# Dummy matmuls of 128 columns instead of 256 in front of the first attention scores

## The chip, the cores and the metric

The kernel runs on one core of a Trainium2 chip. The metric is the time of one execution in device microseconds (us). A profiled execution also has a span, from its first to its last recorded instruction, which is about 1.7 us shorter than its time. Ratios are the mean time of one kernel's fast runs over that of the other's of the same rounds, so they are not quite the ratio of the medians quoted. The line numbers L286, L472 and so on are the kernel's own; all kernels here keep them.

## The reference

Causal attention with 16 extra "beacon" keys and values per head, then a two-layer network with a squared relu:

```python
# q, k, v: (8 batches, 8 heads, 576 tokens, 64); beacon_k, beacon_v: (8, 8, 16, 64)
k_all = concat([beacon_k, k]); v_all = concat([beacon_v, v])
scores = q @ k_all.T / 8          # causal mask on the part of k
out = softmax(scores) @ v_all
x = out as (4608 tokens, 512)
h = relu(x @ w_in)                # w_in 512 x 2048
return (h * h) @ w_out            # w_out 2048 x 512, float32
```

## The kernel before

The kernel plans itself before it emits anything: a small simulator walks over all operations with guessed durations and fixes the order of each engine. Where TensorE has nothing ready before 22 us of simulated time, the simulator puts a dummy matmul ("fill"), whose guessed length is 107 ns whatever its size. The order is then frozen, and TensorE keeps to it on the chip: in all ten profiles without a reordering its 3114 other matmuls come in the same sequence of lines.

```python
if best is None:                                   # nothing ready on this engine
    if e == "PE" and 0.3 < now < self.FILL_UNTIL and self.pools["ps"]:
        cols = 128 if now < 4.0 else 256
        free[e] = now + 0.107
        issued.append((Op("fill", "PE", 0.107, lambda e, cols=cols, bank=...: self.fill(bank, cols)), e, now))
...
def emit_fill(bank, cols):                          # L286
    nc.tensor.matmul(ps[bank][:, 0:cols], g[1][:, 0, 0:128], g[1][:, 0, 0:cols], start=True, stop=True)
```

Batch 0's q and k arrive head pair by head pair. Pair 0 comes in two pieces by way of a float32 buffer and a cast (their transposes are L472). Pairs 1 to 3 of batch 0, and all of batch 1, are loaded by GpSimd's queue with a cast on the way (issue L440) and transposed by TensorE (L475). The order of that queue is fixed too:

```python
SOFT = "t0 p1k p1q t1 p2k p2q v0 v1 p3k p3q v2 v3 v4 w0 w1 w2 w3".split()   # p: pair, v: value block, w: quarter of w_in
...
strided[1, 0, 0, "k"].behind[:] = chain[-1:]        # batch 1's first k comes after w3
```

The other lines that matter here: L611 scores, L620 exp, L715 attention times v, L878 first layer of the network, L894 and L896 relu, L903 square, L916 second layer, L318 casts and copies.

The softmax here doesn't subtract the row's maximum and nothing guards it: scores larger than these inputs give would overflow.

## Time and profile before

| | |
|---|---|
| time, median of the first 3 runs | 340.99 us (340.25 to 341.39) |
| execution that was profiled | 342.69 us, span 341.0 us |
| TensorE busy | 335.6 us, 98% |
| dummy matmuls | 83, of which 32 with 128 and 51 with 256 columns |

The profiled execution took longer than any of the timed ones. The rows on which the argument rests are in the prediction. They are rows of the timeline (start, duration, engine, line, operation, output<-inputs, and in brackets the idle time before them with what ended it) and of the chain that ended last (start, duration, what).

### The profile page before, as it was taken

The page shows a single profiled execution, that of the slowest core. Times are in us where ns is not written, and L with a number is a line of the kernel's source. Part 1 is how long each engine was busy: PE and PEld are TensorE (multiplying, and loading weights), DVE is VectorE, ACT ScalarE, POOL GpSimd, SP SyncE. Part 2 cuts the span into 40 slices and gives each one's busy share as a digit, 9 for nine tenths or more (in the row PEclk, how much of TensorE's full clock was granted, in tenths as well). Part 3 has the DMA queues.
Part 4 walks back from the last instruction along what each step waited for, and adds up shares of the span by engine and source line. Part 5 has one row for each costly group of instructions (what it writes and reads, how often), then busy time and mean ns, then how long its engine had stood idle before and what let it go on. Part 6 is the DMA issues. An engine that isn't in the chain of part 4 may idle for free.

```text
span 341.0 us, 7787 instructions
## 1 busy us (share of the span) xinstructions
PE 335.6 (98%) x3197; PEld 187.4 (55%) x3197; DVE 173.0 (51%) x389; ACT 190.3 (56%) x270; POOL 92.5 (27%) x145
## 2 busy tenths in 40 slices
PE   8999999999999999999999999999999999999996
PEld 7677665544564555555467855545454544444444
DVE  3886886238465982477336743767255502401400
ACT  2886765367647765576456653675367316514721
POOL 9773712406504533042315041504000000000000
PEclk9999999999999999999999999999999999999999
DMA  8999987999999999799989998997310131011003
GB/s 143 209 185 213 209 149 165 224 241 217 170 204 238 219 172 189 162 238 188 201 154 220 226 215 131 217 233 125 105 62 2 29 104 62 0 60 65 0 2 123
DMA packets 143953, 51.72 MB, mean 152 GB/s; under 512 B 130702, under 2 KB 138798, under 8 KB 143918
## 3 DMA queue, kind: packets, MB, share of 16 engines
q1 hardware_dynamic: 135375, 42.19, 61.8%
q0 software_dynamic: 7904, 8.69, 15.0%
q8 instruction: 25, 0.41, 0.5%
q10 hardware_dynamic: 639, 0.36, 0.4%
q14 instruction: 10, 0.08, 0.1%
HBM read 37.22 MB, written 9.44 MB: 137 GB/s over the span
## 4 chain that ended last, share of the span: by engine, by line
PE 97%; DVE 1%; issue 0%; ACT 0%; DVEq 0%
PE ps L878 36%; PE ps L916 36%; PE ps L715 9%; PE strip L611 9%; PE ps L286 3%; PE ps L475 2%; PE ps L782 1%; PE ps L828 1%; DVE g L903 1%; PE ps L472 0%; ACT g L894 0%; PE ps L420 0%; DVE g L896 0%; ACT osb L316 0%; DVE g L292 0%
## 5 line engine op out<-in xcount | busy, mean ns | idle before, releaser
L878 PE MATMUL ps<-xT,w_in 128*128 128x512 bf16 (+3 forms) x704 | 134.0, 340 | 0.7 <-DVE g L896 0.7
L916 PE MATMUL ps<-w_out,g 128*128 128x512 bf16 x560 | 131.4, 379 | 0.0
L620 ACT ACTIVATE pt<-strip 128x1024 bf16<-128x1024 f32 (+3 forms) x107 | 101.9, 1000 | 43.2 <-PE strip L611 42.8
L878 PEld LDWEIGHTS <-w_in 128*128 128x128 bf16 x704 | 65.5, 98 | 52.9 <-issue 2.0
L894 ACT ACTIVATE g<-ps 128x512 bf16<-128x512 f32 (+2 forms) x120 | 67.5, 563 | 45.2 <-PE ps L878 44.7
L903 DVE TENSOR_TENSOR g<-g 128x1024 bf16<-128x1024 bf16 (+2 forms) x80 | 54.2, 684 | 68.6 <-ACT g L894 67.7
L916 PEld LDWEIGHTS <-g 128*128 128x128 bf16 x560 | 51.0, 98 | 54.8 <-issue 1.7
L318 POOL CAST qk_area<-stg 128x512 bf16<-128x512 f32 (+2 forms) x60 | 40.1, 676 | 66.1 <-DMA stg<-in_q_dram 33.7
L318 POOL CAST vb<-stg 128x512 bf16<-128x512 f32 (+1 forms) x40 | 26.4, 671 | 67.8 <-DMA stg<-in_v_dram 49.3
L316 ACT COPY osb<-ps 128x512 f32<-128x512 f32 (+2 forms) x28 | 15.8, 567 | 50.8 <-PE ps L916 48.6
L715 PEld LDWEIGHTS <-pt 128*128 128x128 bf16 (+1 forms) x960 | 35.7, 98 | 11.0 <-issue 2.1
L715 PE MATMUL ps<-vb,pt 128*128 128x65 bf16 (+1 forms) x960 | 39.8, 194 | 0.0
L689 DVE TENSOR_TENSOR pt<-pt,tri 128x512 bf16<-128x512 bf16 x64 | 31.6, 503 | 10.2 <-ACT pt L620 9.0
L611 PE MATMUL strip<-qT,kT 64*128 64x208 bf16 (+15 forms) x596 | 34.2, 239 | 0.0
L734 DVE TENSOR_TENSOR xn<-ps,rcp 128x320 bf16<-128x320 f32 (+2 forms) x64 | 31.5, 492 | 2.3
L611 PEld LDWEIGHTS <-kT 64*128 64x128 bf16 x596 | 19.0, 94 | 21.2 <-issue 19.9
L732 DVE RECIPROCAL rcp<-ps 128x5 f32<-128x5 f32 (+2 forms) x64 | 12.2, 190 | 34.5 <-PE ps L715 34.2
L896 DVE TENSOR_SCALAR g<-ps 128x512 bf16<-128x512 f32 (+2 forms) x40 | 23.4, 601 | 8.6 <-PE ps L878 7.4
L318 DVE COPY osb<-ps 128x512 f32<-128x512 f32 (+1 forms) x10 | 6.5, 651 | 31.0 <-PE ps L916 19.0
L286 PE MATMUL ps<-g 128*128 128x256 bf16 (+1 forms) x83 | 12.0, 302 | 1.1 <-DVE warm L293 1.1
L362 POOL DMA_DIRECT2D stg<-in_v_dram x10 | 8.6, 866 | 6.4 <-DMA w_in<-in_moe_w_in_dram 5.3
L286 PEld LDWEIGHTS <-g 128*128 128x128 bf16 x83 | 7.9, 122 | 3.5 <-issue 1.5
(40 smaller groups left out, 82.2 us busy)
## 6 DMA issues: line engine op xcount, KB each, us to landing
out_dram<-osb SPq DMA_DIRECT2D x17, 512.0 KB, 4.3
stg<-in_q_dram SPq DMA_DIRECT2D x24, 256.0 KB, 5.0
stg<-in_k_dram SPq DMA_DIRECT2D x18, 256.0 KB, 5.3
stg<-in_v_dram SPq DMA_DIRECT2D x18, 256.0 KB, 4.7
w_in<-in_moe_w_in_dram POOLq DMA_DIRECT2D x4, 512.0 KB, 8.7
w_out<-in_moe_w_out_dram POOLq DMA_DIRECT2D x4, 512.0 KB, 11.2
stg<-in_v_dram POOLq DMA_DIRECT2D x6, 256.0 KB, 8.3
stg<-in_k_dram SPq DMA_DIRECT2D x6, 224.0 KB, 4.1
```

Of the source, the lines that this page charges most:

```text
L286: nc.tensor.matmul(ps[bank][:, 0:cols], g[1][:, 0, 0:128], g[1][:, 0, 0:cols], start=True, stop=True)
L318: eng[e].tensor_copy(dst, src)
L611: nc.tensor.matmul(st[:, hj, at:at + t1 - t0], kT[b % 2][hp, pr, 128 * c:128 * c + 128], qT[b % 2][hp, pr, t0:t1], start=True, stop=True,)
L620: nc.scalar.activation(pt[:, :, at:at + width], strips[qk.slots[s]][:, :, 0:width], AF.Exp, bias=0.0, scale=scale)
L689: nc.vector.tensor_tensor(out=d, in0=d, in1=tri[:, m0:m0 + m, :][:, None].to_broadcast([128, 2, m, 128]), op=ALU.min)
L715: nc.tensor.matmul(a[:, at + (t - tl[0]) * (D + 1):at + (t - tl[0] + 1) * (D + 1)], P[0:rr, hj, o:o + 128], vb[b % 2][0:rr, c, 2 * pr + hj ...
L734: nc.vector.tensor_tensor(out=xn[b % 2].rearrange("p t (h d) -> p h t d", d=D)[:, h0:h0 + nh, tl[0]:tl[0] + nt], in0=a[:, :, :, 0:D], in1= ...
L878: nc.tensor.matmul(h[:, lo - spans[0][0]:hi - spans[0][0]], w_in_sb[:, mc, ft * 128:(ft + 1) * 128], xT[:, mc, lo % RING:lo % RING + hi - lo],
L894: nc.scalar.activation(dst, h, AF.Relu, bias=0.0, scale=1.0)
L896: nc.vector.tensor_scalar(out=dst, in0=h, scalar1=0.0, scalar2=None, op0=ALU.max)
L903: nc.vector.tensor_tensor(out=d, in0=d, in1=d, op=ALU.mult)
L916: nc.tensor.matmul(o, G[:, fc, ts * 128:(ts + 1) * 128], w_out_sb[:, fc, :], start=(fc == 0), stop=(fc == NFT - 1))
```

## The change

The intent is to get real work onto TensorE sooner. A dummy that already stands in the queue must finish before real work behind it can start, so shorter dummies should delay it less. The diff is one line; in the frozen order it makes 18 dummies shorter: fifteen before the second piece's transposes and three after the first scores.

```diff
-                            cols = 128 if now < 4.0 else 256
+                            cols = 128 if now < 7.0 else 256
```

## The prediction

> **What bounds the kernel now.** I read the page first: it says what the 341 us are made of, but it cannot price a change that touches only the first 9 us.
>
> ```profile
> PE 335.6 (98%) x3197; PEld 187.4 (55%) x3197; DVE 173.0 (51%) x389; ACT 190.3 (56%) x270; POOL 92.5 (27%) x145
> L286 PE MATMUL ps<-g 128*128 128x256 bf16 (+1 forms) x83 | 12.0, 302 | 1.1 <-DVE warm L293 1.1
> ```
>
> TensorE is busy nearly all the time, so over the whole kernel its work is the bound. L286 is the dummy matmul: 83 of them. They keep TensorE occupied while the first loads come in, so the early part of "PE busy" is not work that anyone waits for, and the page cannot tell whether a shorter dummy shortens anything. For that I took the timeline of the first 10 us, where each row is start, duration, engine, instruction, and in brackets the idle time before it and what ended it.
>
> ```profile
> 4.41 0.46 PEld L472 LDWEIGHTS <-qk_area 120*128 120x128 bf16 x4
> 4.84 0.51 ACT L316 CAST qk_area<-osb 112x384 bf16<-112x384 f32 x1 [0.44 <-DMA osb<-in_q_dram]
> 5.25 2.58 PE L286 MATMUL ps<-g 128*128 128x256 bf16 x15
> 5.61 0.36 DVE L318 CAST qk_area<-osb 112x384 bf16<-112x384 f32 x1
> 7.67 0.46 PE L472 MATMUL ps<-ident,qk_area 112*128 112x112 bf16 x6
> 8.17 0.51 DVE L318 COPY kT<-ps 128x336 bf16<-128x336 bf16 x1 [1.79 <-PE ps L472]
> 8.44 0.78 ACT L620 ACTIVATE pt<-strip 128x736 bf16<-128x736 f32 x1 [3.09 <-PE strip L611]
> ```
>
> Fifteen dummies stand between the transposes of the first piece of q and k (L472 at 4.41) and those of the second (L472 at 7.67). The second piece is cast by 4.84 + 0.51 = 5.35 (ScalarE) and 5.61 + 0.36 = 5.97 (VectorE). From 5.97 to 7.67 those transposes wait for nothing but the dummies queued ahead of them: **1.70 us too late**. VectorE idles 1.79 us and ScalarE 3.09 us for it. So in this stage the dummies do bound.
>
> The next question is how far a lead made here travels. The chain that ended last, in order of time, is where I looked (start, duration, what), with the timeline's rows at the same place, and the landing times of the loads.
>
> ```profile
> 27.81 2.64 PE ps L878 x24
> 30.45 0.02 issue
> 30.47 0.41 ACT g L894
> 30.88 0.03 issue
> 30.91 0.70 PE ps L475 x24
> ```
>
> ```profile
> 30.91 0.57 PEld L475 LDWEIGHTS <-qk_area 96*64 96x64 bf16 x24 [0.77 <-DMA qk_area<-in_k_dram]
> 32.57 0.31 PEld L475 LDWEIGHTS <-qk_area 96*64 96x64 bf16 x12 [0.22 <-DMA qk_area<-in_q_dram]
> ```
>
> At 30.91 TensorE starts to transpose batch 1's k. The chain names an activation that freed a PSUM bank at 30.88; the timeline names the load. Both hold: that load was issued at 19.77 and took 11.1 us to land, 19.77 + 11.1 = 30.87. The two end within 0.01 us. The row at 32.57 is the same for q: issued at 20.44, 11.9 to land, 32.34, and TensorE idled for it too. **These two landings are a floor**: TensorE executes in program order, so nothing after 30.9 can start sooner unless batch 1's loads land sooner.
>
> **What the Trainium skill says.** "TensorE: Matmul & The Clock Gate", section "Part 1: The HAM clock gate", says the array starts at half clock and reaches full clock after a free-running window of about 3.4 us with activity, and that back-to-back matmuls start N/1.2 ns apart cold and N/2.4 + 2.5 ns warm: 107 and 213 ns cold, 56 and 109 warm, for 128 and 256 columns. The trace agrees: the 32 early dummies of 128 columns start 107 ns apart; of the fifteen with 256, seven start 213 ns apart (7 start from 5.44 to 6.72) and those from 6.9 on 109. The row of granted clocks (all 9s) does not show this; the spacing does, and the change of pace is at about 6.9 us. "Part 4: PE-mode transpose" of the same page says transposes do not count as activity in the same way; nothing in this trace tests it. "DMA: Bandwidth & Descriptors", section "Issuing engines are not separate DMA queues", says that every queue shares the same DMA engines; here their mean busy share is over 1.0 from 2 to 38 us in the stretches I asked for (1.03, 1.12, 1.11, 1.17, 1.30, 1.12) at some 180 to 230 GB/s, so the loads set their own pace.
>
> **The change part by part.** The comparison of instruction orders shows the same number of instructions on every engine, in the same order; 18 dummies change from 256 to 128 columns: all fifteen above, and the first three of the four after the first scores (8.33 us). Nothing is removed and no wait is added.
>
> 1. The fifteen. From 5.25, at 107 ns each while the clock is cold, they take 15 x 0.107 = 1.6 us: the second transposes start at about 6.85 instead of 7.67, **0.8 us sooner** (both operands have been there since 5.97, so none of this is lost yet). First scores and first exp follow: the exp at about 7.6 instead of 8.44.
> 2. The three of the next group run warm: 3 x (109 - 56) = **0.16 us**. Lead at the first pair-1 transposes: 0.97, that is 7.9 instead of 8.87.
> 3. Then the loads of batch 0's later heads take it back. Landings, as issue plus time to landing: pair 1 k at 2.39 + 4.0 = 6.4 and q at 7.2 (needed at 7.9 and 8.9: no wait); pair 2 k at 4.28 + 5.4 = 9.7 and q at 10.2 (needed at 10.97 - 0.97 = 10.0 and 10.66: just in time); pair 3 k at 7.81 + 6.9 = **14.7** and q at 8.46 + 6.8 = 15.3. Pair 3's k transposes started at 15.08 before, and would now be asked for at 14.1: they wait for 14.7. About **0.35 us** of lead is left.
> 4. Those 0.35 us pass through attention and the first hidden-layer matmuls (L878) to 30.4. There the floor at 30.87 stands: the batch-1 load is issued by GpSimd, whose work before it (casts of v, loads of w_in) waits for loads and not for TensorE. Lead left after 30.91: 30.91 - 30.87 = **0.04 us**, and after 32.57 about zero.
>
> The sum: 0.8 + 0.16 gained, 0.6 lost at 14.7, the rest lost at 30.9. What remains is 0 to 0.05 us of 341, which nobody can see against runs of 340.25 to 341.39.
>
> **The rivals.**
> - *The lead survives.* If the landing at 30.87 moved with the front (earlier casts on GpSimd, or VectorE's copies no longer colliding with GpSimd's descriptor work), 0.35 to 1 us would come through: about 340.0 to 340.6. Against it: busy DMA engines throughout, and the copies only move, they do not shrink. For it: the clock's window is free-running, so in some executions the fifteen run cold to the end (15 x 213 = 3.2 us instead of 2.4), TensorE reaches 30.9 after the landing, and there the change does gain a few tenths. This is why I put the median slightly below the old one.
> - *The clock warms later.* If 128-column dummies or the transposes that now come earlier count as too little activity, the window that closes near 6.9 fails and half clock lasts another 3.4 us. Work between 6.9 and 10.3 would then be up to twice as long, perhaps 1 us, more than the lead: TensorE arrives up to a few tenths behind the floor, 341.0 to 341.5. Against it: the first 32 dummies were 128 columns wide and just as dense, and the array is still filled without a break until 6.85.
> - *ScalarE is the bound and not the loads.* From 9.97 to 14.3 five exps run back to back. If they set the pace, the lead comes through to 14.7 as whole; pair 3's landing still stops it. Same total.
>
> **Range and chances.** Centre: 340.99 less about 0.15 for the executions with an unlucky window, 340.8. The three earlier runs spread over 1.1 us and a second chip session can shift the median by as much, so 340.1 to 341.5. Faster by 2% would need 6.8 us, seven times the whole lead; slower by 2% would need a clock that stays cold for some 14 us. Both 0.01.
>
> **What would show each step right or wrong.** In the changed kernel: (1) the fifteen dummies start 107 ns apart and the second L472 starts at 6.7 to 6.95; (2) the first exp at about 7.6; (3) L475 for pair 3 starts 0.2 to 0.5 us sooner than 15.08, with a landing at about 14.7 just before it; (4) L475 of batch 1 starts at 30.9 again, TensorE now idle longer than 0.47 us before it, the chain naming the load and no activation; from there each stage at its old time within the jitter of landings. Wrong would be: L472 of the second piece waiting for anything other than the dummies; dummies at 107 ns long after 6.9; batch 1's landing moved by more than 0.3 us, in which case the end moves with it; or a span that moves while 30.91 does not, for which I have no mechanism.

## The result, and the profile after

The changed kernel took 340.51 us in the median (340.16 to 340.65, 4 runs) beside 341.1 us for the kernel before, ratio 0.9985 with a 95% interval of 0.9966 to 1.0005: the same. It lies inside the range, 0.3 us under the centre.

The profile, however, fell from a span of 341.0 to 338.4 us, far more than the times did. These are the page's lines for the whole span of the changed kernel:

```profile
PE 333.8 (99%) x3197; PEld 186.2 (55%) x3197; DVE 172.8 (51%) x389; ACT 190.5 (56%) x270; POOL 94.3 (28%) x145
L286 PE MATMUL ps<-g 128*128 128x128 bf16 (+1 forms) x83 | 10.3, 278 | 1.1 <-DVE warm L293 1.1
```

Dummies cost 1.7 us less (10.3 for 12.0), yet the span lost 2.5 (340.95 and 338.45 before rounding). The timeline of the same execution:

```profile
5.22 1.01 PE L286 MATMUL ps<-g 128*128 128x128 bf16 x15
5.52 0.36 DVE L318 CAST qk_area<-osb 112x384 bf16<-112x384 f32 x1
6.07 0.46 PE L472 MATMUL ps<-ident,qk_area 112*128 112x112 bf16 x6
6.83 0.78 ACT L620 ACTIVATE pt<-strip 128x736 bf16<-128x736 f32 x1 [1.68 <-PE strip L611]
9.39 0.31 PEld L475 LDWEIGHTS <-qk_area 96*64 96x64 bf16 x12 [0.41 <-DMA qk_area<-in_k_dram]
10.48 0.31 PEld L475 LDWEIGHTS <-qk_area 96*64 96x64 bf16 x12 [0.60 <-DMA qk_area<-in_q_dram]
26.51 2.78 PE L878 MATMUL ps<-xT,w_in 128*128 128x240 bf16 x24
29.23 0.56 PEld L475 LDWEIGHTS <-qk_area 96*64 96x64 bf16 x24 [0.23 <-DMA qk_area<-in_k_dram]
```

There are three things to read here. First, the second transposes start at 6.07 and not 7.67: 1.6 us sooner, twice the forecast. In this execution the fifteen dummies start 56 ns apart, so the clock was already warm when they began; in the profile of the kernel before it warmed only near 6.9 us. Half of the 1.6 us is therefore the change and half is the clock's luck. Second, the loads of pair 2 (k at 9.39, q at 10.48) now stop TensorE, where it never waited before. The idle times in brackets are those of the weight loads (PEld) and are no measure of this: some 0.2 us stood in each place before without any wait (0.21 and 0.17, "issue"). The starts are a better one: the lead was 1.77 us at pair 1's k (7.10 for 8.87) and 1.15 at pair 2's q (10.48 for 11.63), so these loads cost 0.62 us. Third, batch 1's transposes started at 29.23 and not 30.91. The load itself landed at 29.17 and not at 30.87, and TensorE came to them at 26.51 + 2.78 = 29.29 (ends of matmuls are modelled), so it did not wait. I had taken that landing as fixed.

The rest of the 2.5 us is a stall further on. The timeline of the kernel before, near 39 us:

```profile
38.88 2.69 POOL L318 CAST vb<-stg 128x512 bf16<-128x512 f32 x4
38.99 2.88 DVE L903 TENSOR_TENSOR g<-g 128x544 bf16<-128x544 bf16 x3
42.27 1.03 PE L878 MATMUL ps<-xT,w_in 128*128 128x272 bf16 x8 [0.69 <-DVE g L896]
```

and of the changed kernel in its first profile:

```profile
36.94 2.91 POOL L318 CAST vb<-stg 128x512 bf16<-128x512 f32 x4
37.34 2.02 DVE L903 TENSOR_TENSOR g<-g 128x544 bf16<-128x544 bf16 x3
```

Three squares need 1.3 us when nothing disturbs them (0.44 each); beside GpSimd's casts they took 2.88 us in one execution and 2.02 in the other. In the slow case TensorE ran out of freed banks and stood still for 0.69 us. The Trainium skill, "SBUF — State Buffer", section "Who interferes with whom", says that a VectorE instruction with two SBUF inputs contends with a GpSimd instruction that reads SBUF. The square reads its input twice from SBUF and the cast reads SBUF, and these numbers agree. Up to the first L916 (46.44 before, 43.94 after) the two executions are 2.50 us apart, 1.68 of it at batch 1 and 0.82 in this stretch; from there to the end they stay 2.5 apart.

So two profiles cannot price this change. The question for the experiments was which of these differences come with the change, and how much of the front's lead reaches the end.

### The profile page after: what moved, and what is told of

Its sections match the earlier page's. It is cut to its first block, busy times and chain, and to the rows that moved or that the text cites. A ratio compares the mean times of both kernels' runs of the same rounds, so it can differ in the third digit from the quotient of the medians.

```text
span 338.4 us, 7787 instructions
## 1 busy us (share of the span) xinstructions
PE 333.8 (99%) x3197; PEld 186.2 (55%) x3197; DVE 172.8 (51%) x389; ACT 190.5 (56%) x270; POOL 94.3 (28%) x145
## 4 chain that ended last, share of the span: by engine, by line
PE 96%; DMA 2%; POOL 1%; issue 0%; ACT 0%; POOLq 0%
PE ps L878 37%; PE ps L916 36%; PE ps L715 9%; PE strip L611 8%; DMA qk_area<-in_q_dram 2%; PE ps L475 1%; PE ps L782 1%; PE ps L286 1%; PE ps L828 1%; POOL qk_area L440 1%; POOL tri L302 0%; POOL tri L300 0%; POOL ident masks.py:199 0%; ACT osb L316 0%; POOL ident masks.py:197 0%
## 5 line engine op out<-in xcount | busy, mean ns | idle before, releaser
L878 PE MATMUL ps<-xT,w_in 128*128 128x512 bf16 (+3 forms) x704 | 133.8, 340 | 0.0
L916 PE MATMUL ps<-w_out,g 128*128 128x512 bf16 x560 | 131.4, 379 | 0.0
L878 PEld LDWEIGHTS <-w_in 128*128 128x128 bf16 x704 | 65.5, 98 | 52.1 <-issue 1.1
L916 PEld LDWEIGHTS <-g 128*128 128x128 bf16 x560 | 51.0, 98 | 54.8 <-issue 1.7
L318 POOL CAST qk_area<-stg 128x512 bf16<-128x512 f32 (+2 forms) x60 | 42.2, 713 | 65.7 <-DMA stg<-in_q_dram 36.0
L689 DVE TENSOR_TENSOR pt<-pt,tri 128x512 bf16<-128x512 bf16 x64 | 30.4, 483 | 10.0 <-ACT pt L620 8.8
L896 DVE TENSOR_SCALAR g<-ps 128x512 bf16<-128x512 f32 (+2 forms) x40 | 23.4, 602 | 9.0 <-PE ps L878 7.9
L286 PE MATMUL ps<-g 128*128 128x128 bf16 (+1 forms) x83 | 10.3, 278 | 1.1 <-DVE warm L293 1.1
L693 DVE TENSOR_TENSOR pt<-pt,tri 80x160 bf16<-80x160 bf16 x32 | 10.2, 320 | 0.0
```

Source lines behind the costliest of these rows:

```text
L318: eng[e].tensor_copy(dst, src)
L689: nc.vector.tensor_tensor(out=d, in0=d, in1=tri[:, m0:m0 + m, :][:, None].to_broadcast([128, 2, m, 128]), op=ALU.min)
L878: nc.tensor.matmul(h[:, lo - spans[0][0]:hi - spans[0][0]], w_in_sb[:, mc, ft * 128:(ft + 1) * 128], xT[:, mc, lo % RING:lo % RING + hi - lo],
L896: nc.vector.tensor_scalar(out=dst, in0=h, scalar1=0.0, scalar2=None, op0=ALU.max)
L916: nc.tensor.matmul(o, G[:, fc, ts * 128:(ts + 1) * 128], w_out_sb[:, fc, :], start=(fc == 0), stop=(fc == NFT - 1))
```

## The experiments

The theory ("F"): batch 1's first transposes start at the later of two times, TensorE's own **arrival** (the end of the L878 group in front of them) and the **landing** of batch 1's k. Both vary from execution to execution, and the change moves only the arrival. The rival "S": the load stream keeps step with the front, so shorter dummies pull the landing forward as well. Other rivals are named in the expectations. All runs gave a correct result.

### The two kernels again

`before_again` and `after_again` are the two kernels unchanged; `after_third` is the changed one once more, in a later session.

> The kernel before, unchanged, timed against itself: the noise of the comparison, and a second profile. Ratio 1.000 within 0.001. In the first profile TensorE's clock warmed at 6.87 us and batch 1's k landed at 30.87. Theory F (the landing of batch 1's k and q is a floor whose time has nothing to do with the dummies; it and the clock's window vary from execution to execution): in this profile both may lie elsewhere, the landing anywhere from 29 to 31, with the end following the landing. Rival S (the loads keep step with the front, so shorter dummies pull the landing forward): the landing stays within 0.3 us of 30.9, since nothing was changed.

> The changed kernel, unchanged, for a tight ratio and a second profile. Theory F: ratio 0.998 to 1.000 (0 to 0.7 us), the landing of batch 1's k at a time that varies as in the kernel before (29 to 31), TensorE idle before it. Rival S: the landing again near 29.2 and the ratio at 0.995 or lower. The second transposes should start at 6.0 to 6.1 if the clock is warm by 5.2, at 6.85 if it is not, against 6.9 and 7.67 or later in the kernel before.

> The changed kernel once more, for its time and a third profile. Theory F: 340.3 to 341.0, ratio 0.9975 to 1.001; batch 1's first transposes start at the later of TensorE's arrival (29.3 to 29.6 as in the two profiles so far) and the landing (29.2 to 30.9 in all profiles so far), within 0.1 us.

Measured: `before_again` 341.07 us against itself at 340.67 (ratio 1.0011, 0.9994 to 1.0027). `after_again` 340.63 (1.0004, 0.998 to 1.0029). `after_third` 340.61 against 340.87 (0.9996, 0.9982 to 1.001). Over all sessions the 16 runs of the changed kernel have a median of 340.53 us, the 43 of the kernel before 340.91: a gain of 0.4 us by medians, and of 0.2 by means (340.75, 340.93). The 0.2 is no more than its standard error, so a gain is not clear of noise.

The profiled `before_again` execution is the slowest of its six (341.97 us), but about 1 us of that has nothing to do with the front: near 197 us TensorE waited for a transposing DMA. Of the other profiles only two have such a wait (0.32 us in `f0`, and 0.61 near 229 us in `early_after`).

```profile
197.12 0.61 PE L611 MATMUL strip<-qT,kT 64*128 64x112 bf16 x10 [1.00 <-DMA kT<-qk_area]
```

Here is its front:

```profile
5.25 2.29 PE L286 MATMUL ps<-g 128*128 128x256 bf16 x15
7.38 0.46 PE L472 MATMUL ps<-ident,qk_area 112*128 112x112 bf16 x6
27.36 2.78 PE L878 MATMUL ps<-xT,w_in 128*128 128x240 bf16 x24
30.07 0.57 PEld L475 LDWEIGHTS <-qk_area 96*64 96x64 bf16 x24 [0.22 <-DMA qk_area<-in_k_dram]
```

and that of `after_third`, where the clock happened to be as cold as in the first profile of the kernel before:

```profile
5.25 1.75 PE L286 MATMUL ps<-g 128*128 128x128 bf16 x15
6.82 0.47 PE L472 MATMUL ps<-ident,qk_area 112*128 112x112 bf16 x6
10.75 0.31 PEld L475 LDWEIGHTS <-qk_area 96*64 96x64 bf16 x12 [0.29 <-DMA qk_area<-in_q_dram]
29.53 0.57 PEld L475 LDWEIGHTS <-qk_area 96*64 96x64 bf16 x24 [0.27 <-DMA qk_area<-in_k_dram]
```

With the clock equally cold the second transposes moved from 7.67 to 6.82, by 0.85 us: this is the change alone. In `before_again` the landing (18.82 at issue, plus 11.2) was 30.02 and TensorE arrived at 27.36 + 2.78 = 30.14, so the arrival set the start. The same kernel thus has either one in front: rival S's first forecast, a landing within 0.3 us of 30.9, is off by 0.9. The load took the same time in both profiles (11.1 and 11.2 us from issue to landing); GpSimd issued it at 19.77 in one and at 18.82 in the other.

### Longer dummies, none, and shorter ones everywhere

`f512` makes the 18 dummies 512 columns wide; `f0` leaves them out with all orders kept; `f128all` makes every dummy 128 wide, up to the last one at 22 us.

```diff
-cols = 128 if now < 4.0 else 256
+cols = 128 if now < 4.0 else 512 if now < 7.0 else 256    # f512 (the 256 columns read twice)
+cols = 128 if now < 4.0 else 0 if now < 7.0 else 256      # f0 (0: nothing is emitted)
+cols = 128 if now < 99.0 else 256                         # f128all
```

> The kernel before with the same 18 dummies at 512 columns in place of 256 (one cause doubled). They cost 15 x 0.107 + 3 x 0.107 = 1.9 us more on a warm clock and up to 3.5 us more on a cold one, all of it between the casts and the second transposes. Theory F with the slack of the change: some of this is swallowed by the slack before batch 1's landing (0 in the first profile, 0.8 where the clock is warm early), the rest comes out at the end: 0.8 to 2 us longer, ratio 1.002 to 1.006, batch 1's k landing still between 29 and 31 and TensorE busy up to its transposes. Rival S: the landing is late by the same 1.9 us and more. Rival N (the first 10 us never matter): ratio 1.000.

> The kernel before with the 18 dummies left out, everything else in the same order. The second transposes start as soon as their casts are done, at about 6.05. Theory F: at most what the change gives, 0 to 0.7 us, ratio 0.998 to 1.000, if the clock stays warm without the dummies. Rival C (the dummies are needed for the clock): TensorE idles about 0.8 us before 6.05, the clock warms or cools a window later, matmuls of 128 columns start 107 ns apart well after 7 us, and the ratio is 1.000 to 1.004.

> Every dummy matmul of 128 columns: 33 more than in the changed kernel, between 8 and 23 us. Theory F: no further gain, ratio 0.998 to 1.001 and within 0.3 us of the changed kernel run beside it, since TensorE already waits for loads between 9 and 15 us and again at batch 1; waits for the loads of pairs 2 and 3 grow. Rival D (dummies still delay attention after 9 us): another 0.5 to 1.5 us, ratio 0.995 to 0.997.

Measured: `f512` 342.66 us, ratio 1.0051 (1.0034 to 1.0068), clearly longer. `f0` 342.36 us, ratio 1.0037 (1.0009 to 1.0065), longer, and scattered from 340.44 to 343.65. `f128all` 340.89 us, ratio 1.001 (0.9988 to 1.0031): nothing gained. The rows at batch 1, first of `f512`:

```profile
29.12 2.78 PE L878 MATMUL ps<-xT,w_in 128*128 128x240 bf16 x24
31.83 0.57 PEld L475 LDWEIGHTS <-qk_area 96*64 96x64 bf16 x24 [0.22 <-issue]
```

then of `f128all`:

```profile
25.95 2.78 PE L878 MATMUL ps<-xT,w_in 128*128 128x240 bf16 x24
28.91 0.57 PEld L475 LDWEIGHTS <-qk_area 96*64 96x64 bf16 x24 [0.46 <-DMA qk_area<-in_k_dram]
28.91 0.70 PE L475 MATMUL ps<-ident,qk_area 96*64 96x96 bf16 x24 [0.17 <-DMA qk_area<-in_k_dram]
```

In `f512` TensorE arrives at 31.90, some 1.2 us after the landing at 30.74; "issue" means that it waited for nothing, and the median is 2.0 us longer (mean 1.7). A delay of the front came through to the end. In `f128all` it arrives at 28.73, about 1.4 us sooner than in `before_again`, and then waits for the load for 0.17 us only, so 1.2 us of that lead pass this point. The profiled execution was indeed the fastest of its six (339.99 us).

That the six together gained nothing has another side in the record. Three of them (341.29, 342.02 and 342.60 us) have a mean granted clock of 0.995, 0.990 and 0.990; the other three (339.99, 340.48 and 340.50) have 0.999 or 1.000, and no execution of any other version is below 0.998. If the clock fell to half, these are 3.4 and 6.8 us at half clock in 340 us (an estimate from the two means). Where it fell, and whether the shorter dummies were the reason, is not shown: none of the three was profiled. At full clock the median is 340.48 us, near the 340.61 of `after_third` in the same session, as F forecast. But `f128all` does not show that a lead of the front is worth nothing.

`f0` missed F's forecast (at most 1.000); its ratio lies in rival C's range, without C's other signs in the profile. TensorE waited 0.56 us for VectorE's cast before the second transposes at 5.88, and as forecast they started as soon as they could. The clock in its profile was warm at 5.66 us and stayed so, which speaks against rival C in this execution. Yet the median is 1.7 us longer. Its profile (342.13 us) shows the landing at 30.09, TensorE held by it for 0.37 us, then 0.3 us lost behind VectorE near 41 us and 0.3 us for the transposing DMA near 197 us. Why four of six executions took over 342 us while two took 340.44 and 340.82 is not explained by that one profile. Rival C is not excluded for them: their mean clocks are 0.999 or 1.000, but this mean leaves out the cold stretch before the first warming (it is 1.00 for the first profile, which was cold until 6.87 us), so a late warming would not show in it.

### The landing moved later

`late_before` and `late_after` add one load of 256 KB to GpSimd's queue between the last quarter of w_in and batch 1's k; its data are never used.

```diff
-    return [nc.gpsimd.dma_start(out=w_in_sb[...], in_=moe_w_in...[...])]
+    return [nc.gpsimd.dma_start(out=w_in_sb[...], in_=moe_w_in...[...])] + (
+        [nc.gpsimd.dma_start(out=osb[1][:, 0, :], in_=moe_w_out[0:128, :])] if i == 3 else [])
```

> The kernel before with one more load of 256 KB (moe_w_out's first rows into an output buffer that is idle then, never read) between the last quarter of w_in and batch 1's k and q; every engine's order is otherwise the same. The stream moves about 195 KB per us there, so all that follows lands some 1.3 us later: batch 1's k at 31 to 32. Theory F (that landing is a floor for TensorE): TensorE idles before batch 1's first transposes and the end moves by 0.7 to 1.5 us, ratio 1.002 to 1.0045. Rival E (TensorE's own arrival sets the end and the landing has slack): ratio 1.000 to 1.001.

> The same extra load in the changed kernel. Theory F: with the landing this late the 0.8 us that shorter dummies save is swallowed whole: the same time as late_before within 0.3 us, the same start of batch 1's first transposes within the variation of the landing (0.5), and 0.8 us more idle time of TensorE before them. Rival E: 0.4 to 0.8 us faster than late_before, as the front's lead comes through.

Measured: `late_before` 341.68 us, ratio 1.002 (0.9997 to 1.0043); `late_after` 342.3 us, ratio 1.0032 (1.0009 to 1.0056). The later landing costs 0.8 and 1.4 us by medians, though `late_before`'s interval just includes zero. The lead of the shorter dummies does not show: the changed version is, if anything, the slower of the two. That speaks against rival E, which had it 0.4 to 0.8 us faster. F's closer forecast, the same time within 0.3 us, was missed (0.6 by medians, with intervals that overlap widely). The row of `late_before`, whose profile is of its slowest execution (342.65 us):

```profile
31.59 0.57 PEld L475 LDWEIGHTS <-qk_area 96*64 96x64 bf16 x24 [1.73 <-DMA qk_area<-in_k_dram]
```

TensorE had arrived at 30.16 and idled for the load. In `late_after`'s profile, its fastest execution (340.88 us), the load landed at 29.95 in spite of the addition, so the two profiles do not show the equal starts that I had forecast. That the late landing hid the lead is thus argued from the times alone.

### The landing moved earlier

`early_before` and `early_after` load batch 1's first k and q ahead of the last quarter of w_in; `wfirst_before` and `wfirst_after` let GpSimd issue all of w_in before it casts the third to fifth v block. The simulator then shifts TensorE's order a little, so each pair is compared within itself.

```diff
-strided[1, 0, 0, "k"].behind[:] = chain[-1:]
+# early: k and q of pairs 0 and 1 behind w2, w3 behind them, the other pairs behind w3
+strided[1,0,0,"k"].behind[:], w_ops["in",3].behind[:], strided[1,0,2,"k"].behind[:] = [w_ops["in",2]], [strided[1,0,0,"q"]], [w_ops["in",3]]
+# wfirst: the line above kept, and the casts of v blocks 2 to 4 behind w3
+[cast[0, "v", c].behind.append(w_ops["in", 3]) for c in range(2, NT)]
```

> The kernel before with batch 1's first k and q (576 KB) loaded ahead of the last quarter of w_in and not behind it; the scheduler moves TensorE's order to suit. They land about 2.5 us sooner (27 to 28.5), the last quarter of w_in about 2.9 us later (near 32.5). Theory F: TensorE does not wait for batch 1's k any more; its arrival sets the start of those transposes. The end: 340 to 342, as the last quarter of w_in may become the next floor.

> The same reordering in the changed kernel. Theory F: with the floor out of the way batch 1's first transposes start 0.6 to 1.0 us sooner than in early_before; at the end 0.4 to 0.9 us remain if no later load takes its place, 0 if the last quarter of w_in does. Rival S (the loads keep step with the front): the landings are 0.8 us sooner too. If this version is faster than both kernels it is the one to keep.

> The kernel before with GpSimd issuing all four quarters of w_in before it casts batch 0's third to fifth v block, so that these issues do not wait for those loads to land (in the profiles the last two quarters are issued at 17.3 to 18.3, after the casts, and the stream thins out near 21 us). TensorE's order shifts a little, 10 dummies more. Theory F (the landing of batch 1's k is a floor set by GpSimd's issue times): issues of w_in at 14.9 and 15.6, that landing 0.3 to 1 us sooner (28.5 to 30), TensorE's arrival as before (30.1 to 30.4) now alone sets those transposes. End 339.5 to 341.5.

> The same reordering in the changed kernel. Theory F: the landing no longer in the way, the 0.8 us of the shorter dummies come through to batch 1's first transposes: 0.5 to 0.9 us sooner than in wfirst_before, and 0.3 to 0.9 us at the end; ratio 0.996 to 0.999. If the gain is again under 0.3 us, another wait (v casts now later, or batch 1's second half of k and q) has taken the place.

Measured, medians beside 340.92 (early) and 340.87 (wfirst) of the kernel before: `early_before` 341.48, `early_after` 341.74, `wfirst_before` 341.65, `wfirst_after` 341.18. None beats the two kernels. Within the pairs the changed dummies gained -0.26 and 0.47 us by medians. Neither is clear of noise: in wfirst the means differ by 0.2 us, and the ratios' intervals (1.0011 to 1.0037 and 1.0005 to 1.003) overlap.

In `early_before` TensorE no longer waits for batch 1's k. In `early_after` those transposes start 0.43 us sooner (26.91 for 27.34), and the next load, q, takes it back:

```profile
26.91 0.31 PEld L475 LDWEIGHTS <-qk_area 96*64 96x64 bf16 x12
28.83 0.31 PEld L475 LDWEIGHTS <-qk_area 96*64 96x64 bf16 x12 [0.82 <-DMA qk_area<-in_q_dram]
```

`wfirst` is the cleaner pair. In `wfirst_before` the landing was at 28.84 and TensorE arrived at 30.10, so the floor was out of the way, as planned. The changed version:

```profile
26.18 2.78 PE L878 MATMUL ps<-xT,w_in 128*128 128x240 bf16 x24
29.03 0.57 PEld L475 LDWEIGHTS <-qk_area 96*64 96x64 bf16 x24 [0.36 <-DMA qk_area<-in_k_dram]
```

It starts 1.00 us sooner (29.03 for 30.03; some of it a warmer clock). At the first L916 0.42 us are left (46.81 for 47.23), and they are still there at the end (spans 339.4 and 339.8; medians 0.47 apart). The missing 0.6 us are a wait again: in `wfirst_after` TensorE stood 0.6 us near 42 us for a relu on VectorE (L896), behind squares that took 2.47 us for three while GpSimd was casting. This stall of L878 behind L896 appeared in four of the twelve profiles with the usual order or the wfirst order (0.7 before, 0.4 `after_third`, 0.3 `f0`, 0.6 `wfirst_after`), where the three squares took 2.47 to 2.88 us. In the other eight they took 1.76 to 2.28 and there was none, but for some 0.25 us in `f128all` (2.28).

### All profiles together

Arrival is the start plus the duration of the last L878 group, landing is issue plus time to landing; ends of matmuls are modelled, so a start can lie up to 0.1 before an arrival. "Second transposes" is L472 at the second piece; "pair 2 q" is the start of those transposes.

| kernel | second transposes | pair 2 q | arrival | landing of batch 1's k | start |
|---|---|---|---|---|---|
| before | 7.67 | 11.63 | 30.43 | 30.87 | 30.91 |
| before_again | 7.38 | 11.34 | 30.14 | 30.02 | 30.07 |
| late_before | 7.40 | 11.35 | 30.16 | 31.52 | 31.59 |
| after | 6.07 | 10.48 | 29.29 | 29.17 | 29.23 |
| after_again | 6.34 | 10.65 | 29.45 | 29.57 | 29.57 |
| after_third | 6.82 | 10.76 | 29.56 | 29.49 | 29.53 |
| late_after | 6.89 | 10.72 | 29.52 | 29.95 | 29.97 |
| f512 | 8.83 | 13.10 | 31.90 | 30.74 | 31.83 |
| f0 | 5.88 | 10.34 | 29.71 | 30.09 | 30.09 |
| f128all | 6.80 | 10.27 | 28.73 | 28.82 | 28.91 |
| wfirst_before | 7.39 | 11.35 | 30.10 | 28.84 | 30.03 |
| wfirst_after | 6.16 | 9.95 | 28.96 | 29.02 | 29.03 |

Two rules hold in this table. The start is the later of arrival and landing, within 0.1 us, in all twelve. And in the first eight rows the arrival follows the transposes of pair 2's q by 18.8 us: whatever lead is there at 10 us reaches 29 us in full. `f128all` needs 18.5, its dummies on the way being shorter, and `f0` 19.4, its pair 3 transposes starting 3.9 us after pair 2's q where the first eight rows have 3.45.

The table also keeps rival S alive in part. With the usual queue order the landing came at 29.2 to 29.6 in the three profiles of the changed kernel and at 30.0 and 30.9 in the two of the kernel before, although GpSimd issued it at 18.8 to 19.2 in four of the five. From issue to landing the load took 9.5 us in `f128all`, 10.3 to 10.5 in the changed kernel, 10.7 in `f0`, 11.1 and 11.2 in the kernel before and 11.4 in `f512`: nearly the order of the arrivals, as rival S has it. The stream itself differs from 20 to 23 us, first in `before_again`:

```profile
20.00:23.00 3.00, 3.00 (x70) 2.25 (x67) 2.60 (x10) 2.50 (x5) 2.89 (x5) 1.00 1.10 162
```

then in `after_again` (the last column is GB/s):

```profile
20.00:23.00 3.00, 3.00 (x75) 2.56 (x74) 2.89 (x11) 2.74 (x4) 2.41 (x4) 1.00 1.24 204
```

In the other profiles it was 159 (before), 150 (late_before), 178 (f512) and 159 (late_after) against 203 (after, after_third), 205 (f0), 187 (f128all) and 204 to 208 (both early and both wfirst). So the thin stretch goes mostly with the slow front, but `late_after` has it with a fast one and the early and wfirst versions lack it with a slow one. Inside those two pairs the landing did not come sooner with the shorter dummies: k of batch 1 at 29.02 against 28.84 in wfirst, at 26.88 against 26.53 in early. What thins the stream stays open (the guess in the prediction, VectorE's copies against GpSimd's descriptor work, was not tested), and so it is not shown that the change moves the arrival alone.

## Why the prediction was right or wrong

The time, 340.51 against 340.8, was right, but it does not prove the account. The range was as wide as the noise, and the measured time lies as well in the band of the first rival, that the lead survives (340.0 to 340.6). What is right at the root: the lead is real, and loads can stop TensorE behind it. That they swallow most of it is not shown. At batch 1's transposes the three profiles of the changed kernel were still 0.5 to 0.8 us ahead of `before_again` (29.23, 29.57 and 29.53 for 30.07). By the prediction's own sign, a landing that moves by more than 0.3 us, its account of this stage was wrong: the landing came 1.3 to 1.7 us before 30.87. Its steps fared unequally.

1. *The fifteen save 0.8 us.* Right: 0.85 with equally cold clocks (6.82 in `after_third`, forecast 6.85; first exp at 7.60, forecast 7.6). The clock warmed at other times in other executions, as the rival had allowed, and this moves the same row by up to 0.8 us.
2. *The next three save 0.16.* Right: from the second transposes to pair 1's k took 1.20 us before (8.87 - 7.67) and 1.03 after (7.10 - 6.07).
3. *Pair 3's landing at 14.7 takes the lead back to 0.35.* Wrong. That landing varies: in the changed kernel's first profile the load, issued at 7.84, took 5.6 us and landed at 13.4, and TensorE did not wait for it. What stopped TensorE was pair 2, which I had called "just in time": it cost 0.62 us in the first profile, where the clock's luck had doubled the lead, and 0.1 in `after_third`. The lead over `before_again` that survives at pair 2's q is 0.6 to 0.9 us (11.34 against 10.48 to 10.76), and it reaches 29 us whole. Pair 3's k did stop TensorE elsewhere, in `f0` (landing at 14.2) and for 0.60 us in `f128all` (13.7).
4. *The landing at 30.87 takes the rest.* Right in kind: the later of landing and arrival set the start in every profile, and with the landing moved later the times show no lead. Wrong in size: the landing is not at 30.87 for every execution but anywhere from 28.8 to 30.9 with the usual queue order, so the lead that passes is 0.5 to 0.8 us in the profiles and not 0.04. Its premise, that the loads set their own pace, is doubtful too: the load was faster where the front was (rival S).
5. *What remains is 0 to 0.05 us, and 0.15 with unlucky clocks.* Perhaps too small: the sessions gave 0.6, 0.0 and 0.3 us by medians, and no interval excludes zero, so this step stays open. An estimate for typical executions fits, but it is no test, as it leaves out the profiles that lost time after batch 1: from the start at batch 1 to the end of the span the undisturbed profiles took about 309.2 us (338.40 - 29.23, 340.90 - 31.59, 339.20 - 29.97), and a time is 1.7 us more, so the median of 340.91 means a start near 30.0 and 340.53 one near 29.6. The first is where the kernel before arrives, the second where the changed kernel's load lands.

Not foreseen was the stall of VectorE behind GpSimd's casts, which cost up to 0.7 us in some executions of either kernel and took 0.6 us of the lead in the one version that had no floor at batch 1. The rival of the late clock did not come true in any profile of the changed kernel: it was warm by 6.84 us at the latest. Some of its executions were slow nevertheless (342.61 and 341.94 in `after_again`) and none of these was profiled, so a late warming is not excluded there. The rival that ScalarE sets the pace did not show: from 8 to 20 us TensorE's matmuls wait for ScalarE in no profile, and in the changed kernel the exps wait for TensorE (0.23 to 0.58 us at a time in `after_third`).

The largest error of method was to read two landing times of one profile as properties of the kernel. The profile was of an execution at 342.69 us, above all of the timed ones.

## What to carry to other kernels

Filler work that has been queued in a fixed order delays what comes behind it, and cutting it pays only as far as the next load that has to land; find that load and compare its landing with the arrival before counting the gain. Here a longer front came through to the end (`f512`, 1.7 to 2.0 us), while the gain of a shorter one was not clear of noise. A test from both sides is cheap, but look at the granted clock of every execution before reading it: in `f128all` half of them had lost some. Before an explanation is built on one profile, compare that execution's time with the other runs, and profile the unchanged kernel a second time.

## What the Trainium skill lacked or had wrong

- "TensorE: Matmul & The Clock Gate", Part 1: spacing cold and warm as stated (107 and 56 ns at 128 columns, 213 and 109 at 256). The page puts the change of pace about 4 us into sustained activity, give or take 0.5 us; here the trace's clock record has it anywhere from 4.95 to 6.87 us after the span's start (profiles of the first and the changed kernel), with dummies from about 1.1 us on, so the spread was twice that. I found no figure there for how busy TensorE must be to keep the clock; in `f128all`, with the shortest dummies, the mean granted clock was 0.990 to 0.995 in three of six executions.
- The same page, Part 4: transposes are said not to count as activity in the same way. No run here tests it by itself; `f0`, with transposes, scores and 0.6 us of idling in place of dummies from 5.3 us on, kept the warm clock in its profile.
- "SBUF — State Buffer", "Who interferes with whom": agrees; it gives no duration for these two instructions side by side. Here three squares that need 1.3 us took 1.76 to 2.88 us beside GpSimd's casts.
- "DMA: Bandwidth & Descriptors": I found no figure there for how much the landing of one queued load varies between executions of one program. Here batch 1's k took 10.3 to 11.2 us from issue to landing in five profiles of the two kernels, and in the kernel before it landed 0.85 us apart (30.02 and 30.87) because GpSimd issued it 0.95 us apart. Both are enough to decide whether TensorE waits.
